# Converting six late weight halves during attention, and loading the feed-forward input in slices from two rings

## The chip, the cores and the metric

The kernel runs on one core of one Trainium2 chip. The metric is the device time of one execution in microseconds (us), as the median of several executions. The engines of the core are named as in the profile: PE (TensorE matmul), PEld (TensorE weight load), DVE (VectorE), ACT (ScalarE), POOL (GpSimd) and SP (SyncE, which here only issues DMAs).

## The reference

Attention over 32 (batch, head) pairs, sequence 1152, head size 64, with the queries averaged in pairs along the sequence; then a feed-forward layer with a leaky activation on the joined heads.

```python
q_pool = q.reshape(B, H, S // 2, 2, D).mean(axis=3)
scores = scale * np.matmul(q_pool, k.transpose(0, 1, 3, 2))
attn = softmax(scores)                                   # written out with max, exp, sum + 1e-9
x = np.matmul(attn, v).transpose(0, 2, 1, 3).reshape(B * S // 2, H * D)     # 2304 x 512
h = x @ w_in                                             # 512 -> 2048
g = np.maximum(h, 0.0) + alpha * np.minimum(h, 0.0)
y = g @ w_out                                            # 2048 -> 512
```

The weights w_in, w_out and alpha are drawn as 64-bit floats; all other inputs are 32-bit.

## The kernel before

**Who orders the work.** All work is added as tasks to a planner (`Scheduler`, L72). A task names its engine, an assumed duration, what it reads and writes, and a priority (the lower number goes first). The planner plays the tasks through in assumed time and emits each engine's instructions in that order; on the chip every engine, and SP's queue of DMA issues, runs its list strictly in order. A `Ring` (L40) is a set of tile buffers; a task that writes a new tile of a ring can start once the users of the buffer's last tile are done.

**Attention.** 32 heads, about 17 us each. For each head `head_prep` (L544) loads queries and keys (rings `r_qs`, `r_kk`), rounds the keys into `r_k1` and makes low parts; `head_max` (L708) finds the row maxima: PE makes blocks of scores `m`, DVE reduces them (`bx`, L812), a last reduction over `bx` (L822) is kept as `maxed[n]`, and the result goes by DMA into the queries (`q<-mm`, L844). `head_main` (L851) makes the scores (L863, L864), their exponentials on ACT (L876), partial sums on POOL and DVE (L891) and the weighted values (L903). `pair_end` (L918) divides by the sums for two heads at a time, splits the result into a high and a low part (`x2`) and stores it to DRAM (`xs`, L981), one DMA of 128 partitions for each head; the partitions are two halves j of the queries by 64 values of the head.

**Feed-forward.** The hidden size 2048 is cut in 16 tiles f. Each product is three matmuls (`mm3`, L383: high weight by high x, high by low, low by high). `hidden` (L390) makes one tile of h from the four slices kd of x (12 matmuls of 288 columns), and ACT and DVE turn it into `gs`. The rows of x are cut in 8 parts (b, j). A low sweep (`low_sweep`, L429) does tiles 0 to 4 of one part, 60 matmuls for h and 60 for y, and stores y to DRAM (`yp`). Low sweeps have priority 1000 and up, below all of attention, and run where attention leaves PE free and after it. A high sweep (`high_sweep`, L453) does tiles 5 to 15 of one part, 132 matmuls for h and 132 for y, adds `yp` and stores the result. The 8 high sweeps come last.

**x.** `x_load` (L370) loads all four slices of one part by two DMAs of 64 partitions each into the one buffer of `r_x` (L355). The next part can be loaded when the last matmul of h has read the old one.

**Weights.** A weight half (f, i) is 128 x 512: i = 0 of w_in, i = 1 of w_out. `w_convert` (L312) loads the 64-bit form (`wraw`, 512 KB, two buffers) and makes a 32-bit number of it, ACT once (`size`, L319), DVE four times (L322, L328, L334, L340); `w_split` (L295) rounds it to the high part on ACT (L301) and makes the low part on DVE (L304). The ten halves of tiles 0 to 4 are converted during heads 2 to 12 or so. The 22 halves of tiles 5 to 15 are added at L1072, after all of attention is emitted, because their tiles lie in a pool (`hpool`, L1070) that takes over the space of attention's pool. Their priority is 2000 - 1 + 0.05 (f - 5), the loads' 1 less: above that of the first high sweep's ACT and DVE work, below that of the low sweeps.

Of the kernel before, what the change touches and what calls it, by code (L numbers as in the profile page):

```python
# [182 lines left out]
def attention_ffn(  # L183
# [30 lines left out]
    Q0: float = 3.069,  # L214
    Q1: float = 2.046,
    G: int = 3,
    J: int = 3,
    AB: int = 7,
    ADDS: tuple = (1, 4, 7),
    R0: float = 1.378,  # L220
    R1: float = 0.7,
    R2: float = 4.009,
# [63 lines left out]
    wh, wl, w_done = {}, {}, {}  # L286
    hpool = [None]

    def w_tiles(f):
        if f not in wh:  # L290
            pool = wpool if f < NLO else hpool[0]
            wh[f] = pool.tile([P, 2 * DMO], F32R, tag=f"wh{f}", name=f"wh{f}")
            wl[f] = pool.tile([P, 2 * DMO], F32R, tag=f"wl{f}", name=f"wl{f}")

    def w_split(f, i, mag, prio):  # L295
        s = slice(i * DMO, (i + 1) * DMO)
        w = Buf()

        def high():
            w_tiles(f)  # L300
            nc.scalar.activation(out=wh[f][:, s], in_=mag.t, func=AF.Copy)  # L301

        def low():
            nc.vector.tensor_tensor(  # L304
                out=wl[f][:, s], in0=mag.t, in1=wh[f][:, s].bitcast(F32), op=ALU.subtract
            )

        t = add(ACT, act(DMO), high, reads=[mag], writes=[w], prio=prio)
        add(DVE, dve(DMO), low, reads=[mag], writes=[w], deps=[t], prio=prio, lock=True)
        w_done[f, i] = w  # L310

    def w_convert(f, i, prio, release=()):  # L312
        raw, mag, bits = Buf(r_raw), Buf(r_mag), Buf(r_bits)

        def load():
            nc.sync.dma_start(out=raw.t.rearrange("p n t -> p (n t)"), in_=wt[f, i].bitcast(I32))

        def size():
            nc.scalar.activation(out=mag.t, in_=raw.t[:, :, 1].bitcast(F32), func=AF.Abs)  # L319

        def top():
# [28 lines left out]
        add(DVE, dve(DMO), value, reads=[bits], writes=[mag], deps=[t0, t3], prio=prio, lock=True)  # L350
        w_split(f, i, mag, prio)


    nal_b = Buf()
    r_x = Ring([P, KD, 2, HQ], F32R, "x", 1)  # L355
    r_pos = Ring([P, HQ], F32, "pos", 3)
    r_neg = Ring([P, HQ], F32, "neg", 2)
    r_gs = Ring([P, 2, HQ], F32R, "gs", NLO + 2)
# [3 lines left out]
    r_h = Ring([P, 512], F32, "h", 1)  # L362
    r_y = Ring([P, 512], F32, "y", 4)
    r_ypt = Ring([P, KD, HQ], F32, "ypt", 2)
    xs = [dt(f"xs{b}", [KD, 2, 2, D, 2, HQ], F32) for b in range(B)]
    xs_b = [Buf() for b in range(B)]
    yp = [[dt(f"yp{b}_{j}", [P, KD, HQ], F32) for j in range(2)] for b in range(B)]
    yp_b = [[Buf() for j in range(2)] for b in range(B)]

    def x_load(b, j, prio):  # L370
        x = Buf(r_x)
        for i in range(2):
            add(
                SP, 600,
                lambda i=i: nc.sync.dma_start(
                    out=x.t[i * D:(i + 1) * D].bitcast(F32).rearrange("d k r q -> d k (r q)"),
                    in_=xs[b][:, i, j].rearrange("k d r q -> d k (r q)"),
                ),
                reads=[xs_b[b]], writes=[x], prio=prio, size=D * KD * 2 * HQ * 4,
            )  # L380
        return x

    def mm3(ps, a, c, lo, first, last):  # L383
        for i, (w, hl) in enumerate(((wh, 0), (wh, 1), (wl, 0))):
            nc.tensor.matmul(  # L385
                out=ps[:, :HQ], lhsT=w[a][:, c:c + P], rhs=lo(hl),
                start=(first and i == 0), stop=(last and i == 2),
            )

    def hidden(f, x, prio):  # L390
        ps, pos, neg, gs = Buf(r_h), Buf(r_pos), Buf(r_neg), Buf(r_gs)
        t = None
        for kd in range(KD):

            def mm(kd=kd):
                mm3(ps.t, f, kd * P, lambda hl: x.t[:, kd, hl, :], kd == 0, kd == KD - 1)

            t = add(PE, 396, mm, reads=[x, w_done[f, 0]], writes=[ps], deps=[t] if t else [], prio=prio,
                    kind="group" if kd else "first")
        add(  # L400
            ACT, act(HQ, True), lambda: nc.scalar.activation(out=pos.t, in_=ps.t[:, :HQ], func=AF.Relu),  # L401
# [25 lines left out]
        return gs  # L427

    def low_sweep(b, j, prio):  # L429
        x = x_load(b, j, prio)  # L430
        g = [hidden(f, x, prio + 0.01 * f) for f in range(NLO)]
        for m in range(KD):
            ps, ys = Buf(r_h), Buf(r_ys)
# [17 lines left out]
            )  # L451

    def high_sweep(b, j, prio):  # L453
        x = x_load(b, j, prio - 1)
        ypt = Buf(r_ypt)
        add(
            SP, 600, lambda: nc.sync.dma_start(out=ypt.t, in_=yp[b][j]),
# [77 lines left out]
    def key_halves(n, k1, deps):  # L535
        for i in range(2):
# [4 lines left out]
                deps=deps[i], uses=[k1], writes=[k3_b[n]], prio=n - 2, size=D * S * 2,  # L541
            )

    def head_prep(n):  # L544
        kk, k1, q1 = Buf(r_kk), Buf(r_k1), Buf(r_q1)
        i = n % 2
# [25 lines left out]
        for j in range(2):  # L572
# [12 lines left out]
            ACT, act(S), lambda: nc.scalar.activation(out=k1.t, in_=kk.t, func=AF.Copy),  # L585
            reads=[kk], writes=[k1], prio=n - KR + 0.1,
        )
        key_halves(n, k1, [k1.writers] * 2)
        add(
            ACT, act(SQ),  # L590
# [260 lines left out]
    def head_main(n, k1, q1, vv):  # L851
# [3 lines left out]
        for c in range(NC):  # L855
            p = Buf(r_p)
            s = slice(c * P, (c + 1) * P)
            for h in range(2):
# [3 lines left out]
                def scores(ps=ps, q=q, s=s):  # L862
# [15 lines left out]
                    ),  # L878
                    reads=[ps], writes=[p], prio=n + (c + 0.5 * h) / NC,
                )  # L880
            if c % J == 0:

                p0, t_acc = p, None
                part = Buf(r_acc)
                acc[n].append(part)
            else:
                a, b = (p0, p) if c % J == 1 else (part, p)
                eng, dur, e = (DVE, dve(2 * HQ), nc.vector) if c in ADDS else (POOL, 2.4 * 2 * HQ + 50, nc.gpsimd)
                t_acc = add(
                    eng, dur,  # L890
                    lambda a=a, b=b, part=part, e=e: e.tensor_tensor(out=part.t, in0=a.t, in1=b.t, op=ALU.add),  # L891
                    reads=[a, b], writes=[part], deps=[t_acc] if t_acc else [], prio=n + c / NC, lock=True,
                )
# [24 lines left out]
    def pair_end(n):  # L918
        ps, rs, rsd, rc, rrd = Buf(r_ps), Buf(r_rs), Buf(r_rsd), Buf(r_rc), Buf(r_rrd)

        def sums():
            for j in range(NC // J):
                for g in (3, 2, 1, 0):
                    nc.tensor.matmul(  # L924
                        out=ps.t[g * 32:(g + 1) * 32, :HQ], lhsT=ones, rhs=acc[n + g // 2][j].t[:, g % 2],
                        start=j == 0, stop=j == NC // J - 1, tile_position=(0, g * 32),
                    )
# [2 lines left out]
            return d.rearrange("g q -> (g q)").rearrange("(p i) -> p i", p=P)  # L930

        e = n + E0
        add(PE, 500 * NC // J, sums, reads=acc[n] + acc[n + 1], writes=[ps], prio=e, col=True, kind="s")
        add(
            ACT, act(HQ, True) + 93,
            lambda: nc.scalar.activation(out=rs.t, in_=ps.t[:, :HQ], func=AF.Identity, bias=eps),
# [11 lines left out]
        for i in range(2):  # L948
            r, x2 = Buf(r_r), Buf(r_x2)
            for h in range(2):  # L950
# [25 lines left out]
                reads=[r], writes=[x2], deps=[t], prio=e, lock=True,  # L976
            )
            b, h = divmod(n + i, H)
            add(
                SP, 600,  # L980
                lambda x2=x2, b=b, h=h: nc.sync.dma_start(  # L981
                    out=xs[b][h // 2, h % 2].rearrange("j d r q -> (j d) r q"), in_=x2.t.bitcast(F32)
                ),
                reads=[x2], writes=[xs_b[b]], prio=e, size=P * 2 * HQ * 4,
            )

    FF = 1000.0
    with ExitStack() as actx:
        ap = actx.enter_context(tc.tile_pool(name="attn", bufs=1))
        for r in (r_kk, r_vv, r_qs, r_k1, r_q1, r_k3, r_bx, r_mm, r_p, r_acc, r_avs, r_rs, r_rc, r_r, r_x2):  # L990
            r.open(ap)
        k2 += [ap.tile([D + 1, S], F32R, tag=f"k2_{i}", name=f"k2_{i}") for i in range(2)]
        q2 += [ap.tile([D + 1, QW], F32R, tag=f"q2_{i}", name=f"q2_{i}") for i in range(2)]
# [2 lines left out]
        with ExitStack() as pctx:  # L996
# [48 lines left out]
            for i in range(2):  # L1045
                for f in range(NLO):
                    r = int(R2 + R3 * f if i else R0 + R1 * f)
                    w_convert(f, i, W2 + W3 * f if i else W0 + W1 * f, [maxed[max(0, r)]])
            for b in range(B):
                for j in range(2):  # L1050
                    low_sweep(b, j, FF + 2 * b + j)
# [11 lines left out]
        r_h.open(ctx.enter_context(tc.tile_pool(name="ps_h4", bufs=1, space=PSUM)), 4)  # L1063
        r_y.open(ctx.enter_context(tc.tile_pool(name="ps_y", bufs=1, space=PSUM)))
        attn = [
            u for r in (r_kk, r_vv, r_qs, r_k1, r_q1, r_k3, r_bx, r_mm, r_p, r_acc, r_avs, r_rs, r_rc, r_r, r_x2)
            for b in r.made for u in b.users
        ]
        sch.run(lambda: all(t.end is not None for t in attn))
    hpool[0] = ctx.enter_context(tc.tile_pool(name="hpool", bufs=1))  # L1070
    r_ypt.open(hpool[0])
    for f in range(NLO, NFF):  # L1072
        for i in range(2):
            w_convert(f, i, 2 * FF + 0.05 * (f - NLO) - 1)
    for b in range(B):
        for j in range(2):
            high_sweep(b, j, 2 * FF + 2 * b + j)
# [49 lines left out]
```

## Time and profile before

| | us |
|---|---|
| median of 3 executions | 945.16 (940.74 to 945.44) |
| the profiled execution: device time | 949.66 |
| its span, first to last instruction | 947.8 |
| PE busy | 887.1 (94%) |
| DVE busy | 623.2 (66%) |
| ACT busy | 512.9 (54%) |
| POOL busy | 172.9 (18%) |

The span is the part that the trace shows; the device time has 1.9 us more around it. Matmuls are pipelined: one shows as about 0.29 us, while back to back they follow each other at less than half of that, so a stretch is better judged by the number of matmuls in it and by the idle times before them than by the busy share. The granted clock is a share of full speed, 2.4 GHz.

### The profile page before, as it was taken

Reading aid. Unit: us, or ns where it says so; the run is one execution under the profiler, and the core shown is the slowest. Engines: PE = TensorE matmul, PEld = TensorE weight load, DVE = VectorE, ACT = ScalarE, POOL = GpSimd, SP = SyncE. Lnnn points to the kernel's source line nnn. Section 1 sums busy time; section 2 is a strip of 40 time slices with the busy share of each in tenths; the row PEclk is TensorE's granted clock in tenths of the full one; section 3 lists DMA queues with packets and bytes.
Section 4 is the critical chain, followed back from the end, with each engine's and each line's share of the span. In section 5 each row is a group of like instructions: output and inputs, shape, how many; then the busy total and the mean of one; then the engine's idle time right before and its main releaser. Section 6 shows DMA issues by size and latency. Waiting matters only on the chain.

```text
span 947.8 us, 16793 instructions
## 1 busy us (share of the span) xinstructions
PE 887.1 (94%) x6271; PEld 747.1 (79%) x6271; DVE 623.2 (66%) x984; ACT 512.9 (54%) x1337; POOL 172.9 (18%) x126
## 2 busy tenths in 40 slices
PE   8899999999989899999999998996899999999998
PEld 6676666667767677766776888986899999999998
DVE  6799999887777688777778426888632332332332
ACT  6577767666756567656665535654532432432432
POOL 3233233323333233223233200000000000000000
PEclk9899999999999999999999999999799999999999
DMA  9657665855584465665424138686033033043030
GB/s 255 152 156 205 186 179 137 221 148 154 124 198 124 114 159 138 143 160 153 126 72 110 52 86 248 186 216 201 25 99 100 2 100 95 7 101 99 3 75 26
DMA packets 58470, 121.69 MB, mean 128 GB/s; under 512 B 11771, under 2 KB 24598, under 8 KB 58390
## 3 DMA queue, kind: packets, MB, share of 16 engines
q1 hardware_dynamic: 56230, 111.78, 43.6%
q0 software_dynamic: 2160, 8.85, 5.4%
q8 instruction: 49, 0.80, 0.4%
q14 instruction: 31, 0.25, 0.1%
HBM read 92.36 MB, written 19.02 MB: 118 GB/s over the span
## 4 chain that ended last, share of the span: by engine, by line
PE 58%; DMA 20%; DVE 15%; issue 3%; ACT 3%; SPq 1%; POOL 0%; DVEq 0%; ACTq 0%; POOLq 0%
PE h L385 18%; PE av L903 10%; PE y L385 9%; DMA x<-xs 7%; PE m L795 6%; PE s L863 6%; PE s L864 5%; DVE bx L812 3%; DMA rsd<-rs 3%; DMA wraw<-wt 3%; PE s L924 2%; DMA r<-rrd 2%; DMA rc<-rsd 1%; DVE mm L837 1%; DVE k L598 1%
## 5 line engine op out<-in xcount | busy, mean ns | idle before, releaser
L876 ACT ACTIVATE p<-s 128x288 f32<-128x288 f32 x576 | 205.0, 409 | 93.2 <-PE s L864 89.3
L385 PE MATMUL h<-x,wh 128*128 128x288 f32 x1024 | 210.7, 299 | 17.8 <-DMA x<-xs 11.5
L891 POOL TENSOR_TENSOR acc<-acc,p 128x576 f32<-128x576 f32 x96 | 153.4, 1598 | 338.8 <-DVE acc L891 159.3
L812 DVE TENSOR_REDUCE bx<-m 128x2 f32<-128x768 f32 x192 | 179.9, 949 | 46.0 <-PE m L795 44.8
L385 PEld LDWEIGHTS h<-x,wh 128*128 128x128 f32 x1024 | 166.0, 191 | 23.0 <-issue 15.1
L863 PE MATMUL s<-q,k 128*128 128x288 f32 x576 | 170.4, 309 | 6.5 <-ACT p L876 6.2
L864 PE MATMUL s<-q,k 65*128 65x288 f32 x576 | 165.0, 300 | 3.6 <-DMA q<-mm 3.6
L903 PE MATMUL av<-p,vv 128*64 128x288 f32 x1152 | 164.3, 421 | 0.3 <-ACT p L876 0.3
L385 PE MATMUL h<-x,wl 128*128 128x288 f32 x512 | 152.0, 297 | 0.0
L385 PE MATMUL y<-gs,wh 128*128 128x288 f32 x704 | 144.5, 299 | 3.9 <-DVE gs L422 3.9
L411 DVE SCALAR_TENSOR_TENSOR pos<-neg,nal,pos 128x288 f32<-128x288 f32 x128 | 69.7, 545 | 107.6 <-ACT neg L406 102.4
L863 PEld LDWEIGHTS s<-q,k 128*128 128x128 f32 x576 | 110.2, 191 | 24.5 <-ACT p L876 11.0
L401 ACT ACTIVATE pos<-h 128x288 f32<-128x288 f32 x128 | 51.8, 404 | 131.6 <-PE h L385 131.3
L795 PE MATMUL m<-k,q 128*128 128x384 f32 (+1 forms) x384 | 108.2, 366 | 13.2 <-DVE bx L812 11.8
L903 PEld LDWEIGHTS av<-p,vv 128*64 128x64 f32 x1152 | 75.1, 138 | 57.7 <-issue 18.2
L385 PEld LDWEIGHTS y<-gs,wh 128*128 128x128 f32 x704 | 114.8, 191 | 4.5 <-DVE gs L422 4.5
L864 PEld LDWEIGHTS s<-q,k 65*128 65x128 f32 x576 | 110.6, 192 | 4.6 <-DMA q<-mm 4.4
L385 PE MATMUL y<-gs,wl 128*128 128x288 f32 x352 | 104.7, 298 | 0.0
L385 PEld LDWEIGHTS h<-x,wl 128*128 128x128 f32 x512 | 97.4, 190 | 0.0
L417 ACT ACTIVATE gs<-pos 128x288 fp32r<-128x288 f32 x128 | 56.9, 444 | 70.9 <-DVE pos L411 70.5
L795 PEld LDWEIGHTS m<-k,q 128*128 128x128 f32 (+1 forms) x384 | 61.9, 194 | 38.3 <-DVE bx L812 16.3
L422 DVE TENSOR_TENSOR gs<-pos,gs 128x288 fp32r<-128x288 f32 x128 | 58.8, 459 | 47.1 <-ACT gs L417 46.8
(69 smaller groups left out, 984.5 us busy)
## 6 DMA issues: line engine op xcount, KB each, us to landing
x<-xs SPq DMA_DIRECT2D x32, 576.0 KB
kk<-kt SPq DMA_DIRECT2D x63, 288.0 KB
wraw<-wt SPq DMA_DIRECT2D x32, 512.0 KB
qs<-qt SPq DMA_DIRECT2D x16, 576.0 KB
vv<-vt SPq DMA_DIRECT2D x32, 288.0 KB
xs<-x SPq DMA_DIRECT2D x32, 288.0 KB
k<-k SPq DMA_DIRECT2D x62, 144.0 KB
qs<-qt POOLq DMA_DIRECT2D x15, 576.0 KB, 6.8
```

The costliest lines, as they stand in the source:

```text
L385: nc.tensor.matmul(out=ps[:, :HQ], lhsT=w[a][:, c:c + P], rhs=lo(hl), start=(first and i == 0), stop=(last and i == 2),)
L401: ACT, act(HQ, True), lambda: nc.scalar.activation(out=pos.t, in_=ps.t[:, :HQ], func=AF.Relu),
L411: lambda: nc.vector.scalar_tensor_tensor(out=pos.t, in0=neg.t, scalar=nal[:, f:f + 1], in1=pos.t, op0=ALU.mult, op1=ALU.add),
L417: ACT, act(HQ), lambda: nc.scalar.activation(out=gs.t[:, 0], in_=pos.t, func=AF.Copy),
L422: lambda: nc.vector.tensor_tensor(out=gs.t[:, 1], in0=pos.t, in1=gs.t[:, 0].bitcast(F32), op=ALU.subtract),
L795: nc.tensor.matmul(out=ms.t[:, i, :JW], lhsT=q1.t[d, PAD + t * P:PAD + (t + 1) * P], rhs=k1.t[d, j * JW:(j + 1) * JW], start=True, stop=True,)
L812: lambda c=c, e=e, step=step, m=len(pair), ms=ms: nc.vector.tensor_reduce(out=bx.t.rearrange("p t j -> p (t j)")[:, c:e + 1:step], in_=ms. ...
L863: nc.tensor.matmul(out=ps.t[:, :HQ], lhsT=k1.t[:, s], rhs=q1.t[:, q], start=True, stop=False)
L864: nc.tensor.matmul(out=ps.t[:, :HQ], lhsT=k2[n % 2][:, s], rhs=q2[n % 2][:, PAD + q.start:PAD + q.stop], start=False, stop=True)
L876: lambda ps=ps, p=p, h=h: nc.scalar.activation(out=p.t[:, h], in_=ps.t[:, :HQ], func=AF.Exp, scale=SCALE),
L891: lambda a=a, b=b, part=part, e=e: e.tensor_tensor(out=part.t, in0=a.t, in1=b.t, op=ALU.add),
L903: nc.tensor.matmul(out=av.t[h * D:(h + 1) * D, :HQ], lhsT=vv.t[:, e], rhs=p.t[:, h], start=(e == 0), stop=(e == NC - 1),)
```

## The change

Three things, with names as in the diff.

1. The first six halves of the late tiles (f = 5, 6, 7, i = 0, 1; `REUSE`) are added with the attention tasks, with priority 31.0 to 31.5 (their loads 1 less). Their first DVE step waits for `maxed[30]`, their rounding on ACT for the rounded keys of the last two heads. They take no new tiles: high and low part go into the two buffers of `r_kk` (f = 5), the two of `r_qs` (f = 6) and two of the three of `r_k1` (f = 7), once the heads that used those are done. These three rings move to the pool that stays open to the end. 16 halves are left for the stage after attention.
2. x comes in four tiles of one slice each, all 128 partitions, one DMA of 288 KB for each slice; `hidden` waits for slice kd alone. `r_x` becomes a ring of five slices (`XB`). `xs` is laid out for it, and `pair_end` stores each head by two DMAs of 64 partitions.
3. The high sweeps with j = 0 take x from a second ring of four slices (`r_xh`) in `hpool`, those with j = 1 from `r_x`.

`J` becomes a pair `JS` chosen by `n >= JH`; with JH = 32 and heads 0 to 31 it stays 3. Its lines, the constants and some lines of layout are left out here.

```diff
-    def w_tiles(f):
-        if f not in wh:
+    def w_tiles(f, i, w):
+
+        if w.ring is None:
             pool = wpool if f < NLO else hpool[0]
...
+            return
+        flat = w.t if len(w.t.shape) == 2 else w.t.rearrange("p t q -> p (t q)")
+        if w.ring.dtype != F32R:
+            flat = flat.bitcast(F32R)
+        wh[f, i], wl[f, i] = flat[:, :DMO], flat[:, DMO:2 * DMO]
+
+    def w_split(f, i, mag, prio, ring, left):
+        w = Buf(ring)
...
+        t = add(ACT, act(DMO), high, reads=[mag], writes=[w], deps=left, prio=prio)
...
-    r_x = Ring([P, KD, 2, HQ], F32R, "x", 1)
+    r_x = Ring([P, 2, HQ], F32R, "x", XB)
+    r_xh = Ring([P, 2, HQ], F32R, "xh", KD)
...
-    xs = [dt(f"xs{b}", [KD, 2, 2, D, 2, HQ], F32) for b in range(B)]
+    xs = [dt(f"xs{b}", [KD, 2, P, 2, HQ], F32) for b in range(B)]
...
+    def x_load(b, j, prio, ring):
+        xk = [Buf(ring) for k in range(KD)]
+        for k, x in enumerate(xk):
+            add(
+                SP, 600, lambda k=k, x=x: nc.sync.dma_start(out=x.t.bitcast(F32), in_=xs[b][k, j]),
+                reads=[xs_b[b]], writes=[x], prio=prio + 0.0001 * k, size=P * 2 * HQ * 4,
+            )
+        return xk
...
+            t = add(PE, 396, mm, reads=[x[kd], w_done[f, 0]], writes=[ps], deps=[t] if t else [], prio=prio,
                     kind="group" if kd else "first")
...
     def high_sweep(b, j, prio):
-        x = x_load(b, j, prio - 1)
+        x = x_load(b, j, prio - 1, (r_xh, r_x)[j] if XH else r_x)
...
+            for j in range(2):
+                d = slice(j * D, (j + 1) * D)
+                add(
+                    SP, 600,
+                    lambda x2=x2, b=b, h=h, j=j, d=d: nc.sync.dma_start(
+                        out=xs[b][h // 2, j, h % 2 * D:(h % 2 + 1) * D], in_=x2.t[d].bitcast(F32)
+                    ),
+                    reads=[x2], writes=[xs_b[b]], prio=e, size=D * 2 * HQ * 4,
+                )
...
+            rings = [r for r in (r_kk, r_qs, r_k1) for i in range(2)]
+            for c in range(REUSE):
+                f, i = NLO + c // 2, c % 2
+                w_convert(f, i, RP + RS * c, [maxed[RM]], rings[c], loads[-2:])
...
     for f in range(NLO, NFF):
         for i in range(2):
-            w_convert(f, i, 2 * FF + 0.05 * (f - NLO) - 1)
+            if (f, i) in w_done:
+                continue
+            w_convert(f, i, 2 * FF + 0.05 * (f - NLO) - HW)
```

## Rows read from the trace of the kernel before

**Rows 1.** The page, busy tenths in 40 slices of the span (23.7 us each).

```profile
PE   8899999999989899999999998996899999999998
```

**Rows 2.** Stages: busy us (instructions) by engine, granted clock, DMA share, GB/s.

```profile
512.00:552.00 40.00, 39.16 (x301) 28.86 (x300) 18.88 (x27) 19.18 (x55) 12.21 (x8) 1.00 0.11 38
...
568.00:644.00 76.00, 68.14 (x480) 65.41 (x480) 58.89 (x114) 43.61 (x107) 0.00 (x0) 0.98 0.78 219
644.00:694.00 50.00, 39.24 (x266) 38.25 (x266) 35.27 (x66) 21.38 (x49) 0.00 (x0) 0.90 0.40 113
694.00:908.00 214.00, 211.39 (x1584) 210.22 (x1583) 73.74 (x155) 73.89 (x198) 0.00 (x0) 1.00 0.26 67
```

**Rows 3.** The chain that ended last: start us, us, what.

```profile
686.05 7.60 DMA x<-xs
...
693.79 8.17 PE h L385 x60
...
908.42 8.17 PE h L385 x60
```

**Rows 4.** Who waited for whom, whole span: us in total, times, longest.

```profile
PE h L385 <- DMA x<-xs: 11.5, 12, 2.2
```

**Rows 5.** PE in order of time, first matmuls of five sweeps; [idle before <-releaser].

```profile
568.39 0.50 PE L385 MATMUL h<-x,wh 128*128 128x288 f32 x2 [1.27 <-DMA x<-xs]
...
587.57 0.50 PE L385 MATMUL h<-x,wh 128*128 128x288 f32 x2 [2.17 <-DMA x<-xs]
...
606.09 0.50 PE L385 MATMUL h<-x,wh 128*128 128x288 f32 x2 [0.89 <-DMA x<-xs]
...
625.07 0.50 PE L385 MATMUL h<-x,wh 128*128 128x288 f32 x2 [1.64 <-DMA x<-xs]
...
644.10 0.50 PE L385 MATMUL h<-x,wh 128*128 128x288 f32 x2 [2.19 <-DMA x<-xs]
```

**Rows 6.** Two short stretches, columns as in group 2.

```profile
590.00:595.00 5.00, 5.00 (x31) 5.00 (x31) 4.89 (x11) 3.55 (x10) 0.00 (x0) 0.76 0.44 141
...
665.00:674.00 9.00, 6.49 (x25) 6.14 (x26) 8.71 (x17) 5.25 (x14) 0.00 (x0) 0.50 0.14 51
```

**Rows 7.** PE in order of time, within the first high sweep.

```profile
657.98 0.41 PE L385 MATMUL y<-gs,wh 128*128 128x288 f32 x1 [2.41 <-DVE gs L422]
...
665.97 0.85 PE L385 MATMUL h<-x,wh 128*128 128x288 f32 x2 [6.26 <-ACT neg L406]
```

**Rows 8.** DVE's groups, 575 to 672 us: busy us, mean ns | idle before.

```profile
L328 DVE SCALAR_TENSOR_TENSOR wbits<-wraw,wbits 128x512 int32<-128x512 int32 x22 | 15.2, 689 | 0.3
...
L422 DVE TENSOR_TENSOR gs<-pos,gs 128x288 fp32r<-128x288 f32 x21 | 9.5, 453 | 0.0
L322 DVE TENSOR_SCALAR wbits<-wraw 128x512 int32<-128x512 int32 x22 | 9.2, 423 | 14.6 <-DMA wraw<-wt 14.5
```

**Rows 9.** ACT's two steps of a conversion, 570 to 680 us: duration ns min/median/max.

```profile
L319 ACT ACTIVATE wmag<-wraw x22: 657/682/705, 575.5 to 667.0; 128x512 f32<-128x512 f32 x22
...
L301 ACT ACTIVATE wh<-wmag x22: 618/632/650, 581.2 to 670.6; 128x512 fp32r<-128x512 f32 x22
```

**Rows 10.** DVE in order of time: ends of conversions 13, 14 and 22.

```profile
641.74 1.47 DVE L304 TENSOR_TENSOR wl<-wmag,wh 128x512 fp32r<-128x512 f32 x2
...
671.29 0.68 DVE L304 TENSOR_TENSOR wl<-wmag,wh 128x512 fp32r<-128x512 f32 x1
```

**Rows 11.** SP's issues in order of time.

```profile
533.41 0.77 SPq L844 DMA_DIRECT2D q<-mm  x1
...
610.27 5.31 SPq L316 DMA_DIRECT2D wraw<-wt  x2
```

**Rows 12.** One DVE line of attention, whole span: duration ns min/median/max.

```profile
L973 DVE TENSOR_TENSOR x<-r,x x32: 439/448/1666, 71.1 to 570.2; 128x288 fp32r<-128x288 f32 x32
```

**Rows 13.** Single microseconds: PE busy, granted clock, DMA share, GB/s.

```profile
607.00:608.00 1.00, 1.00 (x9) 1.00 1.05 424
...
691.00:692.00 1.00, 1.00 (x10) 1.00 1.05 200
```

More of the change, by code (lines that the diff above doesn't have):

```diff
@@ L216, in attention_ffn @@
     G: int = 3,
-    J: int = 3,
+    JS: tuple = (3, 9),
+    JH: int = 32,
     AB: int = 7,
-    ADDS: tuple = (1, 4, 7),
+    ADDS: tuple = ((1, 4, 7), (1, 4, 7)),
     R0: float = 1.378,
@@ L234, in attention_ffn @@
     COL: float = 0.099,
+    HW: float = 1.0,
+    XB: int = 5,
+    REUSE: int = 6,
+    XH: int = 1,
+    RP: float = 31.0,
+    RS: float = 0.1,
+    RM: int = 30,
 ):
@@ L287, in attention_ffn, with w_convert @@
     hpool = [None]
-    def w_tiles(f):
-        if f not in wh:
+    def w_tiles(f, i, w):
+        if w.ring is None:
             pool = wpool if f < NLO else hpool[0]
[L292 to L297, printed above, removed]
+            wh[f, i] = pool.tile([P, DMO], F32R, tag=f"wh{f}_{i}", name=f"wh{f}_{i}")
+            wl[f, i] = pool.tile([P, DMO], F32R, tag=f"wl{f}_{i}", name=f"wl{f}_{i}")
+            return
[5 more added lines that the diff above has]
+        w = Buf(ring)
         def high():
-            w_tiles(f)
-            nc.scalar.activation(out=wh[f][:, s], in_=mag.t, func=AF.Copy)
+            w_tiles(f, i, w)
+            nc.scalar.activation(out=wh[f, i], in_=mag.t, func=AF.Copy)
         def low():
             nc.vector.tensor_tensor(
-                out=wl[f][:, s], in0=mag.t, in1=wh[f][:, s].bitcast(F32), op=ALU.subtract
+                out=wl[f, i], in0=mag.t, in1=wh[f, i].bitcast(F32), op=ALU.subtract
             )
-        t = add(ACT, act(DMO), high, reads=[mag], writes=[w], prio=prio)
+        t = add(ACT, act(DMO), high, reads=[mag], writes=[w], deps=left, prio=prio)
         add(DVE, dve(DMO), low, reads=[mag], writes=[w], deps=[t], prio=prio, lock=True)
         w_done[f, i] = w
-    def w_convert(f, i, prio, release=()):
+    def w_convert(f, i, prio, release=(), ring=None, left=()):
         raw, mag, bits = Buf(r_raw), Buf(r_mag), Buf(r_bits)
@@ L350, in w_convert @@
         add(DVE, dve(DMO), value, reads=[bits], writes=[mag], deps=[t0, t3], prio=prio, lock=True)
-        w_split(f, i, mag, prio)
+        w_split(f, i, mag, prio, ring, left)
     nal_b = Buf()
-    r_x = Ring([P, KD, 2, HQ], F32R, "x", 1)
+    r_x = Ring([P, 2, HQ], F32R, "x", XB)
+    r_xh = Ring([P, 2, HQ], F32R, "xh", KD)
     r_pos = Ring([P, HQ], F32, "pos", 3)
@@ L368, in attention_ffn @@
     yp_b = [[Buf() for j in range(2)] for b in range(B)]
-    def x_load(b, j, prio):
-        x = Buf(r_x)
-        for i in range(2):
-            add(
[L374 to L379, printed above, removed]
+    def x_load(b, j, prio, ring):
+        xk = [Buf(ring) for k in range(KD)]
+        for k, x in enumerate(xk):
+            add(
+                SP, 600, lambda k=k, x=x: nc.sync.dma_start(out=x.t.bitcast(F32), in_=xs[b][k, j]),
+                reads=[xs_b[b]], writes=[x], prio=prio + 0.0001 * k, size=P * 2 * HQ * 4,
             )
-        return x
+        return xk
     def mm3(ps, a, c, lo, first, last):
@@ L385, in mm3 @@
             nc.tensor.matmul(
-                out=ps[:, :HQ], lhsT=w[a][:, c:c + P], rhs=lo(hl),
+                out=ps[:, :HQ], lhsT=w[a, c // DMO][:, c % DMO:c % DMO + P], rhs=lo(hl),
                 start=(first and i == 0), stop=(last and i == 2),
@@ L395, in mm @@
             def mm(kd=kd):
-                mm3(ps.t, f, kd * P, lambda hl: x.t[:, kd, hl, :], kd == 0, kd == KD - 1)
-            t = add(PE, 396, mm, reads=[x, w_done[f, 0]], writes=[ps], deps=[t] if t else [], prio=prio,
+                mm3(ps.t, f, kd * P, lambda hl: x[kd].t[:, hl, :], kd == 0, kd == KD - 1)
+            t = add(PE, 396, mm, reads=[x[kd], w_done[f, 0]], writes=[ps], deps=[t] if t else [], prio=prio,
                     kind="group" if kd else "first")
@@ L429, in low_sweep @@
     def low_sweep(b, j, prio):
-        x = x_load(b, j, prio)
+        x = x_load(b, j, prio, r_x)
         g = [hidden(f, x, prio + 0.01 * f) for f in range(NLO)]
@@ L542, in key_halves @@
             )
+    loads = []
     def head_prep(n):
@@ L587, in head_prep @@
         )
+        loads.append(k1.writers[-1])
         key_halves(n, k1, [k1.writers] * 2)
@@ L880, in head_main @@
                 )
+            J = JS[n >= JH]
             if c % J == 0:
@@ L887, in head_main @@
                 a, b = (p0, p) if c % J == 1 else (part, p)
-                eng, dur, e = (DVE, dve(2 * HQ), nc.vector) if c in ADDS else (POOL, 2.4 * 2 * HQ + 50, nc.gpsimd)
+                eng, dur, e = (DVE, dve(2 * HQ), nc.vector) if c in ADDS[n >= JH] else (POOL, 2.4 * 2 * HQ + 50, nc.gpsimd)
                 t_acc = add(
@@ L921, in sums @@
         def sums():
+            J = JS[n >= JH]
             for j in range(NC // J):
@@ L932, in pair_end @@
         e = n + E0
-        add(PE, 500 * NC // J, sums, reads=acc[n] + acc[n + 1], writes=[ps], prio=e, col=True, kind="s")
+        add(PE, 500 * NC // JS[n >= JH], sums, reads=acc[n] + acc[n + 1], writes=[ps], prio=e, col=True, kind="s")
         add(
@@ L978, in pair_end @@
             b, h = divmod(n + i, H)
[L979 to L985, printed above, removed]
+            for j in range(2):
[7 more added lines that the diff above has]
+                )
     FF = 1000.0
@@ L989, in attention_ffn @@
         ap = actx.enter_context(tc.tile_pool(name="attn", bufs=1))
-        for r in (r_kk, r_vv, r_qs, r_k1, r_q1, r_k3, r_bx, r_mm, r_p, r_acc, r_avs, r_rs, r_rc, r_r, r_x2):
+        for r in (r_kk, r_qs, r_k1):
+            r.open(fpool if REUSE else ap)
+        for r in (r_vv, r_q1, r_k3, r_bx, r_mm, r_p, r_acc, r_avs, r_rs, r_rc, r_r, r_x2):
             r.open(ap)
@@ L1065, in attention_ffn @@
         attn = [
-            u for r in (r_kk, r_vv, r_qs, r_k1, r_q1, r_k3, r_bx, r_mm, r_p, r_acc, r_avs, r_rs, r_rc, r_r, r_x2)
+            u for r in (*(() if REUSE else (r_kk, r_qs, r_k1)), r_vv, r_q1, r_k3, r_bx, r_mm, r_p, r_acc, r_avs, r_rs, r_rc, r_r, r_x2)
             for b in r.made for u in b.users
@@ L1071, in attention_ffn @@
     r_ypt.open(hpool[0])
+    if XH:
+        r_xh.open(hpool[0])
     for f in range(NLO, NFF):
         for i in range(2):
-            w_convert(f, i, 2 * FF + 0.05 * (f - NLO) - 1)
+            if (f, i) in w_done:
+                continue
+            w_convert(f, i, 2 * FF + 0.05 * (f - NLO) - HW)
     for b in range(B):
```

## The prediction

> **What bounds the kernel now.** I read the page's slices first: PE is at 9 tenths nearly everywhere, with its one deep dip at 6 tenths around 640 to 687 us [rows 1]. So the question is where PE, the busiest engine, stands still, and the next view is a table of stages [rows 2], read by the number of matmuls. From 694 to 908 us there are 1584, which is six high sweeps of 264, at full clock. From 644 to 694 us, the first high sweep, there are 266 in 50 us. Third, the chain: the second high sweep's first matmul is at 693.79 us and the eighth's at 908.42 us [rows 3], so a steady high sweep takes 214.63 / 6 = 35.77 us. The list of waits gives what x costs: 12 waits of h on the load of x, 11.5 us in total [rows 4]; five of them stand before sweeps that begin from 568 to 644 us and sum to 8.16 us [rows 5], which leaves 3.34 us for the seven steady boundaries, 0.48 us each. A steady high sweep without its wait is thus 35.29 us, or 133.7 ns for a matmul; this is PE's floor.
>
> **The first high sweep** starts at 644.10 us [rows 5] and the next at 693.79 us, 49.69 us, that is 13.9 us above a steady one. Inside it PE waits 2.41 us for a `gs` of DVE and 6.26 us for ACT to clear a bank of h [rows 7], and after that it runs at a granted clock of 0.50, the level of 1.2 GHz, from 665 to 674 us, where it stood still before [rows 6]. ACT and DVE are late because conversions come first in their order. The 14th of 22 ends at 643.2 us and the 22nd at 672.0 us [rows 10]: eight remain when the sweep begins, one each 28.8 / 8 = 3.6 us. PE's cover at the sweep's start, with matmuls that need no epilogue, is from 644.1 to the wait that ends at 657.98 us, less its 2.41 us: 11.5 us.
>
> **The low sweeps** that start from 568.39 to 644.10 us take 75.71 / 4 = 18.93 us each against 120 x 133.7 ns = 16.04 us at the floor. Of the excess, 11.6 us in four, 6.89 us are waits for x [rows 5], some 1.2 us a stretch at clock 0.76 after one of them, (1 - 0.76) x 5 us [rows 6], and 3.5 us small waits for `gs`.
>
> **The change, part by part.**
>
> Six halves leave the stage after attention. 14 were done when the first high sweep began; 16 are now wanted in all. If the loads keep their rhythm, two remain, 2 x 3.6 = 7.2 us, under the cover of 11.5 us. The low sweeps get shorter by the parts below, about 9 us in 76, so that time for some 9 / 5 = 2 fewer conversions passes: four remain, 14.4 us, which is 2.9 us past the cover. I take 1.0 us of the 13.9 us as staying, because the last halves belong to tile 15, which PE needs last; ends 0 and 5 us. **Term 1: 12.9 us.**
>
> x in slices. In the low sweeps slice 0 of the next part fits the fifth buffer, and slices 1 to 3 are freed 12 matmuls from the end of h; then 60 matmuls of y, 8.0 us, hide their load. Three slices are 885 KB. At the 200 GB/s of the present x loads alone [rows 13] they move in 4.4 us, at the 424 GB/s of the `wraw` loads [rows 13], whose rows cover all 128 partitions as the new slices do, in 2.1 us. The chain's x load, 7.60 us from the second issue [rows 3], is 1.7 us longer than 1180 KB at 200 GB/s, so 3.8 to 6.1 us and 1.8 us for three issues: 5.6 to 7.9 us, under 8.0 us at both ends. I take the wait as gone, and with it the clock's 1.2 us: 8.16 + 1.2. **Term 2: 9.4 us** (up to 12.9 us if the small waits go too, since h of the next part can then fill them).
>
> Second ring. In the high sweeps x of the next part is loaded a whole sweep ahead, so the seven waits go. Next late is PE itself. **Term 3: 3.3 us.**
>
> What it costs. Six conversions enter the end of attention: 6 x (0.42 + 4 x 0.69) = 19.1 us of DVE [rows 8] and 6 x (0.68 + 0.63) = 7.9 us of ACT [rows 9]. Where they go, 512 to 552 us, DVE has 40 - 18.9 = 21.1 us free, ACT 20.8 us, and DMA is at 0.11 [rows 2]; the 3.1 MB that they load come out of a stage at 0.78. PE is busy 39.16 us of those 40, with low sweeps between the heads. These are the cover; without it the 19.1 us of DVE would lie before head 31's scores. But engines run in order: a conversion step that has just begun holds up a `bx` reduction or an exponential by up to 0.69 us, and the last head has some 13 such steps in a row (six blocks of maxima, two more reductions, the issue of `q<-mm`, the sums), 9 us at most. Attention's end also delays the other 16 halves. Ends: -1 us (slices also spare the low sweeps inside attention a wait) and 9 us. I take 1.5 us, near the low end, because PE has other work at hand there.
>
> POOL is a second cost of that place. One DVE line with two inputs took 0.44 us at least and 1.67 us at most [rows 12], and POOL is busy 12.2 us in 512 to 552 [rows 2]. Four of a conversion's five DVE steps have two inputs. The Trainium skill (SBUF — State Buffer, section Who interferes with whom) says that such a step and a GpSimd instruction that reads SBUF exclude each other for a whole instruction. By that rule the conversions' 24 steps could wait for at most those 12.2 us, an estimate of 31 us of DVE for 21 us of room, and attention would end some 10 us later, which is about the upper end taken above.
>
> Issues. 32 more loads of x at some 0.6 us and 32 more stores of `xs` at 0.4 us are 32 us of SP's time over the whole span. I cost them at nothing: SP only issues DMAs, and 32 us are 3% of its span; if each stood before a load that PE waits for, they would be 0.5 us a time. Moved past other work are six `wraw` loads, now in SP's queue between the loads and stores of the last heads. With two buffers, four of them wait for a buffer. After attention two such issues held the queue for 5.31 us [rows 11]. Behind them stand `q<-mm` of head 31 and the four small transfers of `pair_end`; head 31's scores and the part x of batch 3 wait for those. Bounds 0 to 2 x 5.31 = 10.6 us; I take 0, as the planner places them when a buffer comes free.
>
> **Sum.** 12.9 + 9.4 + 3.3 - 1.5 = 24.1 us, from the profiled execution's 949.66 us: 925.6 us. The median of the runs shown is 945.16 us, 0.9953 of the profiled one; times that, 921.2 us.
>
> **The rivals.**
>
> *The slices come late.* In the low sweeps x waits as before, since two loads of `wraw` of 512 KB share the DMA engines (the stage's share is 0.78 [rows 2]): 885 KB + 1049 KB at 200 GB/s are 9.7 us, past the 8.0 us of y. For it: each of the five waits stood in this stage, and the seven quiet ones are only 0.48 us. Against: one slice of four is there already. Term 2 falls away: 949.66 - 14.7 = 935.0 us, as a median 930.5 us. The Trainium skill (SBUF — State Buffer, section The DMA setup-cost knee) speaks for this rival: each transfer pays about 2 us whatever its size, and one should join transfers. By its fit four slices one after the other would be an estimated 10.7 us where two loads were 6.7 us; but no row here shows loads of one queue following each other in that way.
>
> *No gain: attention gives it back.* All bounds of cost at once (9 us of DVE and ACT steps, 10.6 us of SP's queue) are 19.6 us, and the conversions that start after attention end later too, so that term 1 loses its 5 us. Against the terms' 25.6 us that leaves 1.0 us: 948.7 us, as a median 944 us. Against: PE's other work in 512 to 552 us.
>
> *Slower: SP's queue.* Slices 1 to 3 each wait for their own buffer in the queue, where before one wait stood for a whole part. Inside attention a low sweep is spread over several heads, so a slice load placed a little early by the planner holds everything behind it: keys, values, `q<-mm`. Three low sweeps and the start of a fourth lie there: some 12 holds. At 2.65 us (half of 5.31 us, [rows 11]) these are 32 us, with the `wraw` loads' 10.6 us 42 us; less 24.1 + 1.5 us of gain, 17 us slower: 966 us, as a median 962 us. It decides from 26 us of holds that lie on the chain of heads. Against: the planner asks for the buffer before it places the load.
>
> *It does not do what it says.* The halves could be placed late, since they rank (31.0) behind head 30 and with head 31. Then terms 2 and 3 stay without term 1: 949.66 - 12.7 = 937 us, as a median 932.5 us.
>
> **How the numbers follow.** Forecast 0.62, slices late 0.14, placed late 0.08: these three are faster by more than 0.5% (4.7 us, about what a measurement of this kernel can tell from no change), 0.84. No gain is the same within 0.5%, 0.10; SP's queue is slower, 0.06. Range: the low end has all excess gone, 13.9 + 12.9 + 3.3 + 1 = 31.1 us, 918.6 us, as a median 914 us. The high end is the late slices with the upper bound of attention's cost, 949.66 - 16.2 + 9 = 942.5 us, as a median 938 us. That holds the first three cases, 0.84. The likeliest alone: 914 to 928 us.
>
> **What would show it.** Right: waits of h on x near zero; steady high sweeps of 35.3 us; six `wraw` loads before 552 us; the first high sweep at 35 to 41 us and no stretch at clock 0.50 in it; low sweeps near 16.9 us; `q<-mm` of head 31 within 2 us of its place. Wrong: waits on x of over 1 us between low sweeps (late slices); gaps of SP before `q<-mm` (queue); the last stores of `xs` after 580 us (attention gives it back).

## The result, and the profile after

The changed kernel takes 916.81 us as a median of four executions (912.13 to 925.46) against 945.30 us: ratio 0.973 (95% interval 0.968 to 0.977). A ratio here is taken over the fast executions of both kernels and is not the quotient of the medians beside it, which is 0.970; by the ratio the gain is 26 us, by the medians 28.5 us. Run again in e9 it took 919.24 us, ratio 0.972 (0.969 to 0.975). The forecast was 921 us. The profiled execution took 914.40 us, with a span of 912.6 us. It lies 2.4 us under its median, as the one of before lay 4.5 us over its own, so the two profiled executions differ by 35.3 us, and their spans by 35.2 us.

The page's slices after, as in [rows 1] (22.8 us each):

```profile
PE   8999999899999999999999999999999999999998
```

The dip is gone. Stages, with columns as in [rows 2]; the last two are six steady sweeps and more:

```profile
512.00:552.00 40.00, 39.97 (x310) 31.61 (x309) 35.19 (x53) 25.68 (x68) 10.18 (x6) 1.00 0.32 92
...
568.00:644.00 76.00, 72.12 (x534) 70.57 (x533) 64.31 (x124) 47.20 (x114) 0.00 (x0) 1.00 0.69 233
644.00:694.00 50.00, 50.00 (x379) 50.00 (x379) 18.50 (x39) 18.67 (x50) 0.00 (x0) 1.00 0.21 67
694.00:908.00 214.00, 214.00 (x1619) 214.00 (x1618) 74.82 (x158) 73.66 (x198) 0.00 (x0) 1.00 0.16 53
```

DVE did 35.2 us of work in 512 to 552 us where it did 18.9 us: the six conversions moved there. From 644 to 908 us PE never stands still in this execution, and the granted clock is 1.00, the level of 2.4 GHz. The list of waits, in the columns of [rows 4], has no wait of h on x any more; the longest single wait of PE's is now this one:

```profile
PE y L395 <- DVE gs L432: 2.9, 1, 2.9
```

The first high sweep's first matmul, found by its weights in a key buffer (`kk`), in order of time, and the first matmuls of the second and the eighth high sweep in the chain:

```profile
625.88 1.34 PE L395 MATMUL h<-xh,kk 128*128 128x288 f32 x9
```

```profile
664.11 7.92 PE h L395 x60
...
873.79 7.92 PE h L395 x60
```

How far PE had come at 552 us shows in the number of matmuls of the stage 0 to 552 us, of before, after and e9 in this order (columns as in [rows 2]):

```profile
0.00:552.00 552.00, 517.78 (x3569) 383.48 (x3570) 437.24 (x611) 354.63 (x932) 172.93 (x126) 0.98 0.58 149
```

```profile
0.00:552.00 552.00, 525.37 (x3621) 391.80 (x3622) 463.36 (x648) 366.22 (x956) 174.53 (x126) 0.98 0.59 155
```

```profile
0.00:552.00 552.00, 522.43 (x3597) 388.30 (x3598) 460.42 (x645) 364.10 (x951) 174.80 (x126) 0.98 0.60 155
```

A steady sweep is (873.79 - 664.11) / 6 = 34.95 us, 132.4 ns a matmul. From these marks, and those of [rows 3, 5], the 35.2 us of the spans split so:

| stretch | before | after | gained | forecast |
|---|---|---|---|---|
| up to 552 us: 52 matmuls more at 132.4 ns | | | 6.9 | -1.5 |
| 552 us to the first high sweep, without those 52 | 92.1 | 73.9 + 6.9 | 11.3 | 9.4 |
| first high sweep to the second | 49.7 | 38.2 | 11.5 | 12.9 + 0.5 |
| six steady sweeps | 214.6 | 209.7 | 4.9 | 2.8 |
| the eighth to the end of the span | 39.4 | 38.8 | 0.6 | 0 |

e9, the same kernel, had 28 matmuls more by 552 us and not 52, and its first high sweep took 40.2 us and not 38.2 us; so 3 us of the first line and 2 us of the third come and go from run to run.

### The profile page after: what moved, and what is told of

Read it like the earlier page. It is cut to its first block, busy times and chain, and to the rows that moved or that the text cites. A ratio compares the mean times of both kernels' runs of the same rounds, so it can differ in the third digit from the quotient of the medians.

```text
span 912.6 us, 16886 instructions
## 1 busy us (share of the span) xinstructions
PE 878.2 (96%) x6271; PEld 742.9 (81%) x6271; DVE 628.6 (69%) x984; ACT 513.4 (56%) x1337; POOL 174.5 (19%) x126
## 4 chain that ended last, share of the span: by engine, by line
PE 77%; DVE 11%; DMA 7%; issue 2%; ACT 2%; SPq 0%; POOL 0%; DVEq 0%; ACTq 0%; POOLq 0%
PE h L395 23%; PE y L395 15%; PE av L917 13%; PE m L808 7%; PE s L876 7%; PE s L877 6%; DVE bx L825 3%; PE s L939 2%; DMA rsd<-rs 2%; DMA wraw<-wt 2%; DVE k L611 1%; DMA k<-k 1%; PE av L1040 1%; PE m L789 1%; DMA rc<-rsd 1%
## 5 line engine op out<-in xcount | busy, mean ns | idle before, releaser
L421 DVE SCALAR_TENSOR_TENSOR pos<-neg,nal,pos 128x288 f32<-128x288 f32 x128 | 71.6, 561 | 98.2 <-ACT neg L416 93.1
L395 PE MATMUL h<-x,wh 128*128 128x288 f32 x576 | 118.1, 298 | 0.0
L395 PE MATMUL y<-gs,wh 128*128 128x288 f32 x512 | 102.8, 296 | 0.0
L395 PEld LDWEIGHTS h<-x,wh 128*128 128x128 f32 x576 | 92.8, 189 | 2.5 <-issue 2.2
L395 PE MATMUL h<-x,wl 128*128 128x288 f32 x288 | 85.0, 295 | 0.0
L395 PEld LDWEIGHTS y<-gs,wh 128*128 128x128 f32 x512 | 82.2, 189 | 0.0
L905 DVE TENSOR_TENSOR acc<-p 128x576 f32<-128x576 f32 x96 | 73.1, 762 | 3.5 <-ACT p L889 2.5
L395 PE MATMUL y<-gs,wl 128*128 128x288 f32 x256 | 75.4, 295 | 0.0
```

Source lines behind the costliest of these rows:

```text
L395: nc.tensor.matmul(out=ps[:, :HQ], lhsT=w[a, c // DMO][:, c % DMO:c % DMO + P], rhs=lo(hl), start=(first and i == 0), stop=(last and i == 2),)
L421: lambda: nc.vector.scalar_tensor_tensor(out=pos.t, in0=neg.t, scalar=nal[:, f:f + 1], in1=pos.t, op0=ALU.mult, op1=ALU.add),
```

## The experiments

Ratios are to the kernel before, run beside each on the same chip; the changed kernel is 0.973, and 0.972 in e9.

**e1: x only.** `REUSE: int = 0`.

> The change without its early conversions: all 22 late halves are converted after attention, x in slices and two rings stay. Theory (the terms add up): x gives its 9.4 us in the low sweeps, some 6 us in the steady ones and what was gained inside attention (7 us), the first high sweep stays at 49 to 50 us: about 930 us, ratio 0.984. Rival (the terms share one bound): the conversions end near 670 us as before whatever PE does, so shorter low sweeps only wait longer in the first high sweep, 60 us or more; only the steady sweeps' gain stays: 938 to 942 us, ratio 0.993 to 0.997.

Measured: 927.21 us, ratio 0.984 (0.980 to 0.988). This is the time of the first theory. The first high sweep lasts from 627.7 us, the first matmul of its line on `xh`, to 676.62 us in the chain, 48.9 us, as before, with the same kind of wait (matmuls by tile: duration ns min/median/max, first and last start; the chain; PE's waits from 552 to 700 us):

```profile
L395 PE MATMUL h<-xh,wh x88: 290/295/442, 627.7 to 668.3; 128*128 128x288 f32 x88
```

```profile
676.62 7.93 PE h L395 x60
```

```profile
PE y L395 <- DVE gs L432: 5.8, 2, 2.9
```

The conversions ended at 660 us, not 672 us: they are no fixed bound. With x quick they are fed sooner: DVE's waits for `wraw` from 560 to 672 us fall from 14.5 to 3.7 us. The early halves are worth 0.984 - 0.972, 11 us, on top.

**e2: early halves only.** The change without its lines on x, `xs` and `r_xh`.

> The kernel before with the six early conversions alone: x in one tile, loaded by two DMAs of 64 partitions, xs stored by one DMA a head, no second ring. Theory: the first high sweep falls from 49.7 to 36 to 38 us, the five waits before the low sweeps (8.2 us) and 0.5 us a steady boundary stay: about 932 us, ratio 0.986. If the 7 us gained inside attention came from the moved rings and the planner's new order and not from x, they show here: 925 us.

Measured: 939.99 us, ratio 0.997 (0.994 to 1.0005). A miss of 8 us, though the first high sweep did shrink as told. Its first matmul, in order of time, and the second sweep's in the chain:

```profile
651.54 0.76 PE L399 MATMUL h<-x,kk 128*128 128x288 f32 x4 [2.57 <-DMA x<-xs]
```

```profile
688.61 8.20 PE h L399 x60
```

37.1 us in place of 49.7 us; but it starts at 651.54 us, 7.4 us later than before [rows 5]. 12.6 - 7.4 = 5.2 us is what the two profiled executions differ by (949.66 and 944.50 us). PE had done 26 matmuls fewer by 552 us than before, 3.4 us; the remaining 4 us are in the low sweeps. PE's waits from 552 us to the first matmul of the first high sweep, before and in e2:

```profile
PE h L385 <- DMA x<-xs: 8.2, 5, 2.2
PE h L385 <- DVE gs L422: 0.4, 2, 0.2
```

```profile
PE h L399 <- DMA x<-xs: 7.6, 4, 3.9
PE h L399 <- ACT gs L431: 1.9, 4, 1.0
PE h L399 <- ACT ys L459: 1.3, 1, 1.3
PE h L399 <- DVE gs L436: 0.9, 2, 0.4
```

In sum PE waits no longer for x than before. The waits for ACT and DVE grow, from 0.4 to 4.1 us, and the granted clock from 568 to 600 us is 0.89 where it was 0.95. What makes ACT and DVE late there is not shown.

The longest wait, 3.94 us, is of a load of x that SP issued at 580.4 us, behind two `wraw` loads of 512 KB issued from 577.5 us and two loads of `ypt` (the stored `yp` of a high sweep) of 576 KB from 579.5 us. Before, the same four were issued from 571.6 and 573.2 us, and x at 576.6 us: they are nearer to x in e2, because the last stores of `xs`, which stand ahead of them, come at 576.3 us and not at 570.3 us.

**e3: one load of 128 partitions.** In the kernel before, one buffer, no early halves; `xs` is laid out and stored as in the change:

```diff
-        for i in range(2):
-            add(SP, 600, lambda i=i: nc.sync.dma_start(out=x.t[i * D:(i + 1) * D]..., in_=xs[b][:, i, j]...), ...)
+        add(SP, 600, lambda: nc.sync.dma_start(out=x.t..., in_=xs[b][:, j]...), ...)
```

> The kernel before with one edit: xs laid out so that the one tile of x is loaded by a single DMA of 128 partitions (1152 KB) in place of two of 64, and stored by two DMAs a head; one buffer, no early conversions. Theory (rate): the load takes about 1.7 + 2.9 us and is hidden under 8 us of y, so waits of h on x fall from 11.5 us to under 2 us and steady sweeps to 35.0 us; the first high sweep still waits for conversions. Rival (prefetch): with one buffer the waits stay at 0.5 us a steady boundary and 1 to 2 us in the low sweeps, 945 us.

Measured: 929.64 us, ratio 0.987 (0.982 to 0.993). There is no wait on x left, with one buffer and nothing loaded ahead. A load in a steady sweep, issued at 669.44 us (PE busy, granted clock, DMA share, GB/s of single microseconds):

```profile
670.00:671.00 1.00, 1.00 (x10) 1.00 0.53 44
671.00:672.00 1.00, 1.00 (x10) 1.00 0.73 217
672.00:673.00 1.00, 1.00 (x10) 1.00 1.01 394
673.00:674.00 1.00, 1.00 (x10) 1.00 1.05 415
674.00:675.00 1.00, 1.00 (x10) 1.00 0.35 127
```

The two loads of 64 partitions in the chain of [rows 3], in the kernel before, and four slices of 128 partitions in the changed kernel, issued from 655.02 us, read:

```profile
688.00:689.00 1.00, 1.00 (x10) 1.00 1.09 306
689.00:690.00 1.00, 1.00 (x9) 1.00 1.02 194
690.00:691.00 1.00, 1.00 (x10) 1.00 1.06 240
691.00:692.00 1.00, 1.00 (x10) 1.00 1.05 200
```

```profile
656.00:657.00 1.00, 1.00 (x10) 1.00 0.80 175
657.00:658.00 1.00, 1.00 (x9) 1.00 1.03 403
658.00:659.00 1.00, 1.00 (x10) 1.00 1.07 387
659.00:660.00 1.00, 1.00 (x10) 1.00 0.59 217
```

The same bytes in rows of the same length go at 387 to 415 GB/s, in one load or in four, where two loads of 64 partitions went at 194 to 306 GB/s, each time with all DMA engines busy. So it is the partitions and not the number of loads. One load takes about 4.5 us, well under the 8 us of y. The first high sweep of e3 still waits:

```profile
PE h L384 <- ACT neg L405: 7.6, 2, 5.9
PE y L384 <- DVE gs L421: 3.1, 2, 1.7
```

**e4: no second ring.** `XH: int = 0`.

> The changed kernel without the second ring: all high sweeps take x from the ring of five. Theory (rate): one slice is there ahead and three of 128 partitions land in 4 to 6 us under 8 us of y, so the steady sweeps stay at 34.9 us and the time at 917 us, ratio 0.973. Rival (the second ring carries term 3): seven boundaries wait 0.5 to 0.8 us each, 3.3 to 5.9 us, 920 to 923 us.

Measured: 914.77 us, ratio 0.967 (0.960 to 0.973): no loss. The second ring does nothing for the time.

**e5: one tile, 128 partitions, early halves.** e2 and e3 together.

> The kernel before with two edits only: the single 128-partition load of x into one buffer (as in e3) and the six early conversions (as in e2); no slices, no ring of five, no second ring. Theory (the rate of the x load frees the rest): it does what the whole change does, first high sweep under 38 us, no waits on x, 915 to 920 us, ratio 0.970 to 0.975, although e2 and e3 alone sum to 0.984. Rival (slices and rings carry the difference between the sum and the whole): 928 us, ratio 0.984.

Measured: 914.44 us, ratio 0.970 (0.966 to 0.974): all of the whole change's gain, from two of its parts. One load of x, issued behind two of `wraw` and two of `ypt`, still made PE wait 4.2 us in the profiled execution, where no wait was expected.

**e6: slices, but by 64 partitions.** In the changed kernel:

```diff
-            add(SP, 600, lambda k=k, x=x: nc.sync.dma_start(out=x.t..., in_=xs[b][k, j]), ...)
+            for i in range(2):
+                add(SP, 600, lambda k=k, x=x, i=i: nc.sync.dma_start(out=x.t[i * D:(i + 1) * D]..., in_=xs[b][k, j, i * D:(i + 1) * D]), ...)
```

> The changed kernel with each slice of x loaded by two DMAs of 64 partitions in place of one of 128; rings, early conversions and stores as changed. Theory (rate): x moves at 200 GB/s again, three slices and the weight loads beside them take 8 to 10 us under 8 us of y, low sweeps wait 0.5 to 2 us each and lengthen, steady sweeps with their whole part ahead stay at 35 us: 920 to 927 us. Rival (prefetch is enough): 917 us, ratio 0.972.

Measured: 918.33 us, ratio 0.973 (0.969 to 0.976). The rival holds: no wait on x, although the DMA share from 568 to 644 us is back at 0.83 (columns as in [rows 2]):

```profile
568.00:644.00 76.00, 72.55 (x518) 70.13 (x517) 60.70 (x115) 46.14 (x109) 0.00 (x0) 0.98 0.83 242
```

So the slow load can be hidden by slices loaded ahead, or made quick (e3, e5, e7). The change does both and needs one.

**e7: ring of four.** `XB: int = 4`.

> The changed kernel with four slices in the ring in place of five, so that no slice of the next part can be there ahead in the low sweeps. Theory (rate): four slices of 128 partitions land in 5 to 7 us under 8 us of y; 917 us, ratio 0.972, as e4. Rival (the fifth buffer carries term 2): waits of 1 us before five low sweeps, 922 us.

Measured: 914.42 us, ratio 0.968 (0.964 to 0.971): the fifth buffer does nothing either.

**e8, e12: conversions in turn.** `HW: float = 0.2` in the changed kernel: the remaining conversions rank 0.2 and not 1.0 ahead of the first high sweep.

> The changed kernel with the late conversions' lead over the first high sweep cut from 1.0 to 0.2 in priority, so that ACT and DVE make each tile's gs before conversions that PE needs 4 or more tiles later. Theory: the one wait that is left in the first high sweep (2.9 us on gs) goes: 914 us. Rival: conversions come late for their own tile, PE waits on wl or wh instead: 917 to 925 us.

> e8 again beside the changed kernel: if the wait of 2.9 us in the first high sweep is what it takes away, it is 2 to 4 us under e9; if e8 differed by chance, they are the same.

Measured: e8 912.10 us, ratio 0.963 (0.958 to 0.968); e12 910.76 us, ratio 0.965 (0.962 to 0.968) beside e9's 0.972 (0.969 to 0.975). Their intervals do not meet: this version beats the changed kernel by 0.7%, 6 us, where 2 to 4 us were expected. The same stage in e9 and in e12:

```profile
568.00:644.00 76.00, 72.36 (x529) 70.13 (x527) 63.24 (x121) 46.12 (x111) 0.00 (x0) 1.00 0.75 244
```

```profile
568.00:644.00 76.00, 75.13 (x553) 73.36 (x552) 63.76 (x125) 48.26 (x117) 0.00 (x0) 1.00 0.71 238
```

24 matmuls more, 3.2 us: the wait for `gs`, 3.0 us in e9, is not there. After that wait, which ends at 644.0 us, the granted clock of e9 falls to 0.50 from 646 to 648 us, the level of 1.2 GHz; from 644 to 650 us e9 and e12 read:

```profile
644.00:650.00 6.00, 5.97 (x33) 5.98 (x34) 5.50 (x12) 4.98 (x15) 0.00 (x0) 0.72 0.02 4
```

```profile
644.00:650.00 6.00, 6.00 (x47) 6.00 (x47) 4.45 (x9) 4.13 (x11) 0.00 (x0) 1.00 0.00 0
```

14 matmuls more, 1.9 us. So the wait cost 5 us there, and e9's first high sweep takes 40.2 us against 35.1 us in e12. In the first trace of the changed kernel the same wait, 2.9 us, was followed by a clock of 1.00. e11, below, gains the same 0.7% on e10.

**e9: the changed kernel again.**

> The changed kernel as it is, again, beside e10 to e12 on one chip: ratio 0.968 to 0.973, a narrower interval.

Measured as told above.

**e10, e11: the same edit for the keys.** In the changed kernel, and in e8's:

```diff
-        for j in range(2):
-            d = slice(j * D, (j + 1) * D)
-            add(SP, 600, lambda d=d: nc.sync.dma_start(out=kk.t[d], in_=kt[n]), ...)
+        add(SP, 600, lambda: nc.sync.dma_start(out=kk.t, in_=kt[n]), ...)
...
-        "kt": k.reshape(B * H, S, D).transpose(0, 2, 1),
+        "kt": twice(k.reshape(B * H, S, D).transpose(0, 2, 1), 1),
```

> The changed kernel with the same edit made to the keys: each head's keys lie twice in the input, and one DMA of 128 partitions loads both copies where two of 64 do now (31 heads, 576 KB each; head 0 as before). By the rate that x showed, a head's load falls from about 3 to 1.5 us of all DMA engines. Theory (only a transfer on the path pays): attention is bound by PE and its chain of maxima, keys come heads ahead, so no difference within 0.5%. Rival: the DMA engines, at 0.6 of their time in attention, hold up q<-mm and x there, and attention ends 3 to 8 us earlier: 909 to 914 us.

> e10 and e8 together. Both small effects add if they are real: 3 us under e10, ratio 0.963 to 0.967.

Measured: e10 919.55 us, ratio 0.974 (0.971 to 0.976) beside 0.972; e11 913.99 us, 0.967 (0.963 to 0.970) beside 0.965. No difference: the DMA share up to 552 us fell from 0.60 in e9 to 0.56 in e10, and in e9 no engine had waited for the keys of heads 1 to 31.

## Why the prediction was right

*The first high sweep (term 1, 12.9 us).* Right in mechanism; 11.5 us by the traces (9.5 us by that of e9), 11 us by e1 against the whole. The sum let 1.0 us stay, but 2.9 us on `gs` stayed, inside the bound of 5 us: conversions still rank before the epilogue. e8 takes that away. The last conversion ends at 641.1 us, 15 us into the sweep, as in the working with four left.

*x (terms 2 and 3, 9.4 and 3.3 us).* Right: the waits are gone, 11.3 us and 4.9 us. Of the two rates that I set as ends the upper is the true one: 387 to 403 GB/s for the slices. The lower, 200 GB/s, was one of the slower microseconds of a load that went at 194 to 306 GB/s. Term 3 was too small, most likely because I took the floor from sweeps that still had the wait: 133.7 ns against 132.4 ns a matmul, 0.34 us a sweep. The 3.5 us that I called small waits for `gs` in the low sweeps were misread: the list of waits has 0.4 us of them (e2, the lines of before). Only the low end of the range used them. That the slices and rings were needed for it was a wrong reading of the change: e4, e5 and e7 show each of them without effect once a load covers 128 partitions. The Trainium skill (SBUF — State Buffer, section Door 1: The DMA port swizzle) says that 64 partitions reach half of the ports that a DMA can use, and the same page (section "Can I just issue two DMAs to hit both halves?") that two such transfers do not add up to one of 128. The traces agree: 194 to 306 GB/s against 387 to 415 GB/s. The other rule of the Trainium skill that the prediction cites, on joining transfers, spoke for the late slices; the traces do not bear it out here. Four loads of 288 KB landed within 5 us of the first one's issue, and not in the estimated 10.7 us, and the kernel takes the same time with them (the changed kernel, 0.972) as with one of 1152 KB (e5, 0.970).

*Attention (1.5 us lost).* The cost was about right, its balance was not. The early halves lengthen the end of attention: from the issue of head 31's `q<-mm` to the last stores of `xs` it is 36.9, 35.5 and 34.7 us without them (before, e3, e1) and 40.9, 38.2, 37.0 and 37.7 us with them (e2, e5, the changed kernel, e9). PE has other work there: from 495 to 552 us it did 12 matmuls fewer in e2 than before and 5 fewer in e5 than in e3, 1.6 us at most. What the sum lacked is a gain: the changed kernel is 28 to 52 matmuls ahead by 552 us, 3.7 to 6.9 us, where the sum had 1.5 us lost. This is the term that was mis-sized, by 5 to 8 us in the two traces of the changed kernel, and by itself it is more than the difference between 24.1 and 28.5 us.

Its cause is open. I had named low sweeps inside attention that are spared a wait, and bounded that by 1 us; but up to 552 us the trace of before has no wait of h on x at all. And x cannot be the whole cause: in the runs of this table it is first loaded between 167 and 175 us, and e1, e3 and e9 are 22 to 26 matmuls ahead before that. The trace of before has a granted clock of 0.55 from 35 to 40 us, where theirs have 1.00.

| matmuls | before | e2 | e1 | e3 | changed | e9 |
|---|---|---|---|---|---|---|
| 0 to 165 us | 947 | 942 | 973 | 969 | 947 | 969 |
| 165 to 552 us | 2622 | 2601 | 2632 | 2651 | 2674 | 2628 |

After 165 us the runs with x quick are 6 to 52 matmuls ahead of before, and e2, without it, is 21 behind. That speaks for some gain from x; its size is not shown by one trace of before.

*The parts are not independent.* The sum added them; on the chip early halves give 2.5 us alone and 11 to 17 us with x quick (e1 to the whole, e3 to e5). The whole came out right because both were there. Alone, the gain in the first high sweep was given back ahead of it: 3.4 us up to 552 us, and 4 us in low sweeps that wait longer for ACT and DVE and run at a lower clock. Why is not shown.

*Luck.* The sum was worked from the profiled execution, and from profile to profile it missed: 24.1 us against 35.3 us, and against 29.9 us with e9's. The profiled execution of before lay 4.5 us over its median and that of the changed kernel 2.4 us under its own. That the forecast of 921 us lies 4 us from the median is in part luck.

*The rivals.* Late slices: no wait of PE on x in any run with slices. Attention gives it back: only in e2, where 7.4 of the 12.6 us were lost ahead of the first high sweep, 3.4 us of them up to 552 us. SP's queue: `q<-mm` of head 31 was issued at 526.2 us in the changed kernel, 7 us before its place of before, and the last stores of `xs` came from 563.2 us. Placed late: six conversions ended by 545 us.

## What to carry to other kernels

A load that is split over 64 partitions twice should be one of 128 before any buffer is added for it: here one such edit did what a ring of five, slices and a second ring did. It pays only where someone waits for the load, which the list of waits tells (x: 11.5 us, and gain; the keys: none, and no gain). When an engine ends late in one stage, move work out of it, but look at what ends later by that move (in e2 the last stores of `xs`, by 6 us), and let work that is due rank ahead of work that is merely early.

## What the runs showed of the hardware

Two loads of 64 partitions, one for each half, ran at 194 to 306 GB/s with a DMA share of 1.02 to 1.09 (before, 688 to 692 us); one of 128 with the same row length at 394 to 415 GB/s with a share of 1.01 to 1.05 (e3). A full DMA share is therefore no sign of a full rate.

Steps of the early conversions that began while POOL was adding took longer. From 530 to 545 us two did, of 13 with two inputs, and the 11 others with two inputs before 530 us took 0.62 to 0.69 us. POOL and DVE in order of time, after:

```profile
533.02 1.73 POOL L905 TENSOR_TENSOR acc<-acc,p 128x576 f32<-128x576 f32 x1 [4.63 <-ACT ys L455]
539.11 1.48 POOL L905 TENSOR_TENSOR acc<-acc,p 128x576 f32<-128x576 f32 x1 [4.36 <-DVE acc L905]
```

```profile
533.52 1.78 DVE L353 SCALAR_TENSOR_TENSOR wmag<-wmag,wbits 128x512 f32<-128x512 f32 x1
...
539.22 1.92 DVE L317 TENSOR_TENSOR k<-wmag,k 128x512 fp32r<-128x512 f32 x1
...
543.89 0.69 DVE L317 TENSOR_TENSOR k<-wmag,k 128x512 fp32r<-128x512 f32 x1
```

Both ended about 0.5 us after POOL's instruction, 1.1 and 1.2 us over the 0.69 us of the others. So what the prediction weighed as a second cost of that place is there, but it is 2.3 us of DVE in all, far from its upper bound of 12.2 us.
